# A cached-attention decode kernel: some rows of the second attention's key products go from VectorE to GpSimd and ScalarE

## The chip, the cores and the metric

One core of one Trainium2 chip. The metric is device microseconds of one execution, as the median of several runs. VectorE is DVE in the profile, ScalarE is ACT, GpSimd is POOL, TensorE is PE, and SP (SyncE) issues nearly all transfers.

## The reference, cut to what matters

Two tokens (one for each of two batch entries) go through attention, a gated MLP, the same attention and the same MLP, with the same caches and weights both times, in fp32:

```
q = (layernorm(x) @ wq).reshape(B, Sq, H, Dh).transpose(0, 2, 1, 3)     # B 2, Sq 1, H 32, Dh 128
p = softmax(einsum("bhqd,bhkd->bhqk", q, k_cache) * Dh ** -0.5)         # Sk 8192
x = x + einsum("bhqk,bhkd->bhqd", p, v_cache).reshape(B, Sq, H * Dh) @ wo
x = x + (gelu(layernorm(x) @ w_gate) * (layernorm(x) @ w_up)) @ w_down
```

Keys and values are 268 MB each, so two attentions load about 1.07 GB of the 1.15 GB that the page counts.

## The kernel before, in words

**Items and parts.** The 64 (batch, head) pairs are cut into 34 items: items 0 to 29 hold two neighbouring heads of one batch entry, items 30 to 33 one head (`ITEMS`, L60). A part is `JC` = 16 cache rows of 128 elements on each of 128 partitions: 2048 elements a partition, 1 MiB. A two-head item has 8 parts of keys and 8 of values, a one-head item 4 and 4. The first attention takes the items from 0 to 33, the second from 33 to 0 (`seq`, L498), so that keys of 32 and 33 and values of 31 to 33, still in memory from the first, aren't loaded again.

**Memory.** One buffer, `space`, is cut into 6 slots of 4 parts; the last one is shared with a ring of four weight places. `Arena` hands out ranges while the program is built. `queue` holds the loads in the order in which `plan_first`, `plan_mlp` and `plan_second` put them there; a load goes out when its range is free, and none passes another, since all are issued by SP in order (`load`, L163). So one load whose range is still in use holds up all that stand behind it.

At the start of the second attention (`plan_second`, L343) come `wq` in nine pieces, item 31's keys into the ring, item 30's keys part by part into the places of item 33's, then item 30's values, item 29's keys and item 28's keys, each into places that items 33, 32 and 31 give up, then item 29's values into the pair of slots 0 and 1 (8 MiB in one load, L362). Slot 0 holds item 30's keys and slot 1 its values until then. After that keys and values of the next items alternate, 8 MiB each, into pairs of slots.

**One part of keys** (`multiply`, L520, and `add_up`, L541). VectorE multiplies all 16 rows with the query, which stands in PSUM (`qp`) on all partitions, in place (L527). GpSimd adds the second half of each row's 128 products to the first (L539), and VectorE sums the 64 that are left into the score `S` (L542). In the first six items of the second attention ScalarE sums rows 12 to 15 itself, by an activation with an accumulator (L532), and GpSimd and VectorE do the other twelve (`own_rows`, L512). For the first and last part of the very first item (`at_once`, L516) GpSimd is left out, and VectorE sums the 12 rows over all 128 elements. `add_up` then frees the part, once ScalarE has read it too.

**Behind the keys.** `peak` (L554) takes the maximum on VectorE and transposes it on TensorE, `highest` reduces it and spreads it again over the partitions, `softmax` (L574) takes the exponents on ScalarE, `total` (L595) sums them on TensorE and inverts on VectorE (L606 for one head, L601 for two), `values` (L617) multiplies weights and value rows on TensorE into `acc` (L628) and frees the value parts, `gather` (L638) and `context` (L648) collect the result, and `divide` (L655) scales it into `oT` on VectorE (L660 or L669).

**The order.** The loop from L699 writes it out: while item n's parts are multiplied, the sums, maximum, softmax and values of the item before it, and gather, context and divide of the one before that, are put between them at fixed parts. Every engine works its instructions off in this order, so an instruction that waits holds up all behind it on its engine. The sums of part k-1 come behind the multiply of part k. `divide` comes at k = 3 (L741).

Of the kernel before, what the change touches and what calls it, by code (L numbers as in the profile page):

```python
# [9 lines left out]
F32 = mybir.dt.float32  # L10
# [5 lines left out]
P = 128  # L16
# [8 lines left out]
JC = 16  # L25
# [97 lines left out]
def decode_layers(ctx, tc, x_in, kc, vc, wq, wo, wg, wu, wd, out):  # L123
# [44 lines left out]
    def cache(key, src, n, slots=None, pieces=None):  # L168

        parts = ITEMS[n].parts  # L170

        def make():
            at = arena.pair(key) if slots is None else arena.slots(key, slots, parts)
            if at is None:
                return False
            lo = 0
            for m in pieces or (parts,):
                load(at[lo], n, src, lo, lo + m)
                lo += m
            ready[key] = dict(enumerate(map(part, at)))  # L180
            places[key] = at
            return True

        queue.append(make)

    def half(key, src, n, k, slot):

        def make():
            at = arena.slots(key, (slot,), 4, k)
            if at is None:  # L190
                return False
            load(at[0], n, src, k, k + 4)
            ready.setdefault(key, {}).update((k + i, part(a)) for i, a in enumerate(at))
            return True

        queue.append(make)
# [146 lines left out]
    def plan_second():  # L343
        for us in WQ[1]:
            half_rows(("wq", 1, us[0]), wq, us, None)
        last = PAIRS - 1
        k63, v63, k62, v62 = ("k", 1, SINGLE[3]), ("v", 1, SINGLE[3]), ("k", 1, SINGLE[2]), ("v", 1, SINGLE[2])
        for k in range(4):
            one(("k", 1, SINGLE[1]), kc, SINGLE[1], k, None)
        for k in range(4):  # L350
            one(("k", 1, SINGLE[0]), kc, SINGLE[0], k, (k63, k))

        for kind, k in (("v", 0), ("v", 1), ("k", 0), ("v", 2), ("v", 3), ("k", 1), ("k", 2), ("k", 3)):
            if kind == "k":
                one(("k", 1, last), kc, last, k, (k62, k))
            else:
                one(("v", 1, SINGLE[0]), vc, SINGLE[0], k, (v63, k))
        for k in range(4):
            one(("k", 1, last), kc, last, 4 + k, (v62, k))
        half(("k", 1, last - 1), kc, last - 1, 0, 5)  # L360
        half(("k", 1, last - 1), kc, last - 1, 4, 4)
        cache(("v", 1, last), vc, last)  # L362
        for n in range(last - 2, -1, -1):
            cache(("k", 1, n), kc, n)
            cache(("v", 1, n + 1), vc, n + 1)
        cache(("v", 1, 0), vc, 0, None, (4, 2, 1, 1))
        for g in groups(1):
            out_rows(1, g)
# [111 lines left out]
    def attention(layer):  # L480
# [19 lines left out]
        def query(n):  # L500

            it = ITEMS[n]
            qb[n] = psum2.tile([P, DH], F32, name="qp")
            for i in range(it.heads):
                h, to = it.h + i, slice(i * HALF, i * HALF + P // it.heads)
                c, r = (h // 4) % 4, h // 16 * B + it.b
                nc.tensor.matmul(  # L507
                    qb[n][to, :], pick[32 * c:32 * c + 4, r:r + 1].to_broadcast([4, P // it.heads]),
                    qsb[32 * c:32 * c + 4, (h % 4) * DH:(h % 4 + 1) * DH], start=True, stop=True,
                )  # L510

        def own_rows(n):  # L512

            return 12 if layer == 1 and n in seq[:6] else JC

        def at_once(n, k):  # L516

            return layer == 1 and n == seq[0] and k in (0, ITEMS[n].parts - 1)

        def multiply(n, k):  # L520

            if k == 0:
                S[n] = work.tile([P, SK * 2 // P], F32, name="S")
            u = t = ready[name("k", layer, n)][k]
            if layer == 0 and n in KEYS_HELD:
                u = ready["products"][k % 2]
            nc.vector.tensor_tensor(  # L527
                out=u, in0=t, in1=qb[n].unsqueeze(1).to_broadcast([P, JC, DH]), op=ALU.mult
            )
            r = own_rows(n)  # L530
            for j in range(r, JC):
                nc.scalar.activation(  # L532
                    u[:, j, :], u[:, j, :], AF.Copy, accum_out=S[n][:, k * JC + j:k * JC + j + 1]
                )
            if at_once(n, k):
                prod[n, k] = u[:, :r, :]
                return
            half = prod[n, k] = u[:, :r, :DH // 2]
            nc.gpsimd.tensor_tensor(out=half, in0=half, in1=u[:, :r, DH // 2:], op=ALU.add)  # L539

        def add_up(n, k):  # L541
            nc.vector.tensor_reduce(  # L542
                out=S[n][:, k * JC:k * JC + own_rows(n)], in_=prod.pop((n, k)), axis=AX.X, op=ALU.add
            )
            if layer == 0 and n in KEYS_HELD:
                if n == N - 1 and k >= 2:
                    done(("products", k - 2))
                return
            key = name("k", layer, n)
            done((key, k))  # L550
            if k == ITEMS[n].parts - 1:
                ready.pop(key)
# [102 lines left out]
        def divide(n):  # L655
            it = ITEMS[n]
            lo = 32 * (it.h % GH)
            r = rinv[n]
            if it.heads == 1:
                nc.vector.tensor_tensor(  # L660
                    out=oT[lo:lo + 32, it.h // GH, :, :, :],
                    in0=po[lo:lo + 32, :, :].unsqueeze(2).to_broadcast([32, GH, 2, B]),
                    in1=r[lo:lo + 32, :].unsqueeze(1).unsqueeze(1).to_broadcast([32, GH, 2, B]),
                    op=ALU.mult,
                )
                return
            for i in range(2):
                to = lo + 32 * i
                nc.vector.tensor_tensor(  # L669
                    out=oT[to:to + 32, it.h // GH, :, :, it.b],  # L670
                    in0=po[lo:lo + 32, :, i:i + 1].to_broadcast([32, GH, 2]),
                    in1=r[lo:lo + 32, i:i + 1].unsqueeze(1).to_broadcast([32, GH, 2]),
                    op=ALU.mult,
                )
# [20 lines left out]
        for lo, hi in ((lead, lead + 2), (2 - lead, 4 - lead)):  # L695
            nc.scalar.activation(qsb[:, lo * DH:hi * DH], acc[:, 0, lo * DH:hi * DH], AF.Copy, scale=rstd)
            if lo == lead:
                query(seq[0])
        for i, n in enumerate(seq):  # L699
            last = i == N - 1  # L700
            if not last:
                query(seq[i + 1])
            p = seq[i - 1] if i else None

            v = {N - 2: None, N - 1: N - 3}.get(i, i - 1) if layer == 0 else i - 1
            a = seq[i - 2] if i > 1 and completes(i - 2) and not (layer == 0 and last) else None

            soon = layer == 1 and i in (1, 4)
            first = layer == 1 and i == 1
            if first:  # L710
                add_up(p, ITEMS[p].parts - 1)
                peak(p)
                highest(p)
                softmax(p)
            for k in range(ITEMS[n].parts):
                multiply(n, k)
                if at_once(n, k) and k == 0:
                    add_up(n, k)
                if k == 1 and first:
                    values(v)  # L720
                    total(p)
                if k == 0 and p is not None and not first:
                    add_up(p, ITEMS[p].parts - 1)
                    peak(p)
                if k == (0 if soon else 1) and p is not None and not first:
                    highest(p)
                    softmax(p)
                if k == 2 and not first:
                    if p is not None:
                        total(p)  # L730
                    if a is not None:
                        gather(a)
                        if p < PAIRS:
                            context(a)
                    if v is not None and v >= 0:
                        values(v)
                    if a is not None and p >= PAIRS:
                        context(a)
                if k > 0 and (n, k - 1) in prod:
                    add_up(n, k - 1)  # L740
                if k == 3 and a is not None:  # L741
                    divide(a)
        n, p = seq[-1], seq[-2]
        add_up(n, ITEMS[n].parts - 1)
        first, second = groups(layer)[:2]
# [128 lines left out]
```

## Time and profile before

| | us |
|---|---|
| median of 3 runs | 2698.55 (2697.79 to 2700.42) |
| the profiled execution | 2699.86 |
| its span, first to last instruction | 2698.0 |
| DVE busy | 1865.5 (69%) |
| POOL busy | 1189.3 (44%) |
| PE busy | 897.0 (33%) |
| ACT busy | 130.9 (5%) |

Transfers: 1155.41 MB, 428 GB/s over the span. In the views, a line is named by its number (L527) and a buffer by the program's name; every part of keys or values is `space`. In a view of instructions the first number is the start and the second the length, in us from the start of the span; in the chain a piece is what the end waited for at that moment. The second attention's first multiply starts at 1394.57 us.

### The profile page before, as it was taken

Reading aid. Unit: us, or ns where it says so; the run is one execution under the profiler, and the core shown is the slowest. Engines: PE = TensorE matmul, PEld = TensorE weight load, DVE = VectorE, ACT = ScalarE, POOL = GpSimd, SP = SyncE. Lnnn points to the kernel's source line nnn. Section 1 sums busy time; section 2 is a strip of 40 time slices with the busy share of each in tenths; the row PEclk is TensorE's granted clock in tenths of the full one; section 3 lists DMA queues with packets and bytes.
Section 4 is the critical chain, followed back from the end, with each engine's and each line's share of the span. In section 5 each row is a group of like instructions: output and inputs, shape, how many; then the busy total and the mean of one; then the engine's idle time right before and its main releaser. Section 6 shows DMA issues by size and latency. Waiting matters only on the chain.

```text
span 2698.0 us, 18267 instructions
## 1 busy us (share of the span) xinstructions
PE 897.0 (33%) x7020; PEld 293.9 (11%) x7020; DVE 1865.5 (69%) x1688; ACT 130.9 (5%) x657; POOL 1189.3 (44%) x526
## 2 busy tenths in 40 slices
PE   1323332333233223334653332333233323322355
PEld 0100010001000000111211110001000100000022
DVE  4877787678777776876039887778767867787740
ACT  0000000000000000000013100000000000000000
POOL 2644454445445444544015454445444544544420
PEclk7656665665666566666666665666566666656667
DMA  9999999999999999999999999999999999999998
GB/s 420 436 433 433 434 435 433 432 433 435 434 433 433 432 432 432 433 429 422 407 388 409 434 428 433 433 435 431 432 435 434 431 435 432 434 434 434 435 420 379
DMA packets 33687, 1155.41 MB, mean 428 GB/s; under 512 B 4008, under 2 KB 4032, under 8 KB 5824
## 3 DMA queue, kind: packets, MB, share of 16 engines
q1 hardware_dynamic: 33560, 1154.24, 99.5%
q8 instruction: 55, 0.90, 0.1%
q14 instruction: 32, 0.26, 0.0%
q10 hardware_dynamic: 40, 0.01, 0.0%
HBM read 1154.23 MB, written 0.00 MB: 428 GB/s over the span
## 4 chain that ended last, share of the span: by engine, by line
DMA 84%; DVE 13%; PE 2%; issue 1%; POOL 0%; SPq 0%; ACT 0%; ACTq 0%; DVEq 0%; POOLq 0%
DMA space<-in_A_k_cache_dram 75%; DVE space L527 8%; DVE S L542 4%; DMA space<-in_B_w_up_dram 3%; DMA space<-in_A_wo_dram 2%; DMA space<-in_A_v_cache_dram 2%; DMA space<-in_B_w_down_dram 2%; DMA space<-in_A_wq_dram 1%; PE acc L628 0%; POOL space L539 0%; DMA space<-in_B_w_gate_dram 0%; PE acc L782 0%; DMA x<-in_A_x_dram 0%; PE acc L487 0%; PE xps L831 0%
## 5 line engine op out<-in xcount | busy, mean ns | idle before, releaser
L539 POOL TENSOR_TENSOR space<-space 128x1024 f32<-128x1024 f32 (+1 forms) x510 | 1185.3, 2324 | 1269.1 <-DVE space L527 1253.2
L527 DVE TENSOR_TENSOR space<-space,qp 128x2048 f32<-128x2048 f32 x512 | 1166.3, 2278 | 597.1 <-DMA space<-in_A_k_cache_dram 571.8
L628 PE MATMUL acc<-space,prz 128*8 128x512 f32 x4096 | 589.0, 738 | 455.7 <-DMA space<-in_A_v_cache_dram 450.9
L542 DVE TENSOR_REDUCE S<-space 128x16 f32<-128x1024 f32 (+1 forms) x512 | 612.4, 1196 | 3.1 <-POOL space L539 3.1
L558 PE MATMUL mT<-ident,m 128*1 128x128 f32 x68 | 25.0, 367 | 806.0 <-DVE m L556 806.0
L628 PEld LDWEIGHTS acc<-space,prz 128*8 128x8 f32 x4096 | 118.0, 103 | 869.4 <-DMA space<-in_A_v_cache_dram 451.8
L587 ACT ACTIVATE nbs<-nb 64x1 f32<-64x1 f32 (+1 forms) x128 | 21.1, 165 | 2230.7 <-PE nb L566 2230.0
L558 PEld LDWEIGHTS mT<-ident,m 128*1 128x1 f32 x68 | 5.4, 79 | 822.9 <-issue 791.7
L653 PE MATMUL po<-of,osb 128*32 128x2 f32 x512 | 41.0, 202 | 130.8 <-DVE osb L644 130.8
L566 PE MATMUL nb<-m,unit 1*128 1x2 f32 (+1 forms) x136 | 39.4, 357 | 124.9 <-DVE m L564 124.9
L473 POOL TENSOR_TENSOR rstd<-ve,mhalf 128x1 f32<-128x1 f32 x4 | 2.2, 550 | 167.0 <-DVE ve L471 167.0
L644 DVE SCALAR_TENSOR_TENSOR osb<-acc,diag,osb 128x128 f32<-128x128 f32 x192 | 67.4, 351 | 6.8
L807 DVE STREAM_TRANSPOSE o<-o 128x288 f32<-128x288 f32 x4 | 2.8, 693 | 92.4 <-ACT o L805 92.4
L598 PE MATMUL tot<-sums,unit 128*128 128x2 f32 x120 | 35.3, 363 | 91.7 <-ACT prz L589 91.7
L507 PE MATMUL qp<-qsb,pick 4*64 4x128 f32 (+1 forms) x256 | 31.3, 306 | 80.1 <-DVE space L527 76.9
L589 ACT ACTIVATE prz<-S,nbs 64x128 f32<-64x128 f32 (+1 forms) x128 | 50.7, 396 | 11.7 <-POOL prz L579 7.5
L653 PEld LDWEIGHTS po<-of,osb 128*32 128x32 f32 x512 | 35.7, 154 | 139.1 <-DVE osb L644 137.8
L566 PEld LDWEIGHTS nb<-m,unit 1*128 1x128 f32 x136 | 33.5, 304 | 146.3 <-DVE m L564 146.3
L477 DVE TENSOR_TENSOR x<-xps,x 128x144 f32<-128x144 f32 x4 | 1.2, 308 | 69.0 <-PE xps L831 39.1
L532 ACT ACTIVATE space<-space 128x128 f32<-128x128 f32 x128 | 38.0, 297 | 64.5 <-DVE space L527 60.8
L598 PEld LDWEIGHTS tot<-sums,unit 128*128 128x128 f32 x120 | 30.1, 312 | 96.9 <-ACT prz L589 96.9
L782 PE MATMUL acc<-space,xt 128*8 128x288 f32 x288 | 31.4, 581 | 18.4 <-DMA space<-in_B_w_up_dram 10.7
(64 smaller groups left out, 345.6 us busy)
## 6 DMA issues: line engine op xcount, KB each, us to landing
space<-in_A_k_cache_dram SPq DMA_DIRECT2D x6, 4096.0 KB
space<-in_A_v_cache_dram SPq DMA_DIRECT2D x6, 4096.0 KB
space<-in_A_wo_dram SPq DMA_DIRECT2D x15, 1152.0 KB
space<-in_A_k_cache_dram SPq DMA_DIRECT2D x16, 1024.0 KB
space<-in_B_w_gate_dram SPq DMA_DIRECT2D x3, 3456.0 KB
space<-in_A_v_cache_dram SPq DMA_DIRECT2D x10, 1024.0 KB
space<-in_A_wq_dram SPq DMA_DIRECT2D x3, 3072.0 KB
space<-in_B_w_gate_dram SPq DMA_DIRECT2D x16, 576.0 KB
```

The costliest lines, as they stand in the source:

```text
L507: nc.tensor.matmul(qb[n][to, :], pick[32 * c:32 * c + 4, r:r + 1].to_broadcast([4, P // it.heads]), qsb[32 * c:32 * c + 4, (h % 4) * DH:(h ...
L527: nc.vector.tensor_tensor(out=u, in0=t, in1=qb[n].unsqueeze(1).to_broadcast([P, JC, DH]), op=ALU.mult)
L532: nc.scalar.activation(u[:, j, :], u[:, j, :], AF.Copy, accum_out=S[n][:, k * JC + j:k * JC + j + 1])
L539: nc.gpsimd.tensor_tensor(out=half, in0=half, in1=u[:, :r, DH // 2:], op=ALU.add)
L542: nc.vector.tensor_reduce(out=S[n][:, k * JC:k * JC + own_rows(n)], in_=prod.pop((n, k)), axis=AX.X, op=ALU.add)
L566: nc.tensor.matmul(mT[n][:, :heads], ones[0:1, :], m1[:, :heads], start=True, stop=True)
L589: nc.scalar.activation(pr[at, lo:].rearrange("p (g e) -> p g e", e=4)[:, 0:it.rows // 2:2, :], s[at, :it.rows].rearrange("p (g r) -> p g r ...
L598: nc.tensor.matmul(tot[:, :it.heads], ones, rs.pop(n), start=True, stop=True)
L628: nc.tensor.matmul(accumulator(n)[32 * c:32 * c + 8, :], pr[:, at:at + 8], t[g // 4][:, g % 4 * 4:g % 4 * 4 + 4, :].rearrange("p j d -> p ...
L644: nc.vector.scalar_tensor_tensor(t, q[:, r, :], diag[:, r:r + 1], t, op0=ALU.mult, op1=ALU.add,)
L653: nc.tensor.matmul(po[lo:lo + 32, i, :], t[:, i::GH], of, start=True, stop=True)
L782: nc.tensor.matmul(acc[32 * c:32 * c + 4 * B, h, :HG], window(u, 4 * g + 2 * e), w[:, k, c, :], start=(key == steps[0][0] and k == 0), sto ...
```

## The change

In the first five items of the second attention (33 to 29) VectorE multiplies rows 0 to 11 of each part, and GpSimd rows 12 to 15. GpSimd doesn't read PSUM, so ScalarE first copies the item's query to `qs` in SBUF, once an item. ScalarE sums rows 9 to 15, GpSimd and VectorE rows 0 to 8; in the two `at_once` parts ScalarE sums rows 11 to 15 and VectorE the other 11. Item 28, which had ScalarE's help before, has none now. Item 29's values come as two loads, parts 0 to 3 into slot 0 and parts 4 to 7 into slot 1, and each waits for its own slot only. Where the item before the one at hand has one head, `divide` moves from k = 3 to k = 1 of the next item (`late`); in the first attention this concerns item 29, in the second item 32.

```diff
-        cache(("v", 1, last), vc, last)
+        half(("v", 1, last), vc, last, 0, 0)
+        half(("v", 1, last), vc, last, 4, 1)
...
-        def own_rows(n):
-
-            return 12 if layer == 1 and n in seq[:6] else JC
+        def waited(n):
+
+            return layer == 1 and n in seq[:5]
...
+        def own_rows(n, k):
+
+            return 11 if at_once(n, k) else 9 if waited(n) else JC
+
+        qs = once.tile([P, 2, DH], F32, name="qs", tag="xc")
...
+            rows = 12 if waited(n) else JC
             nc.vector.tensor_tensor(
-                out=u, in0=t, in1=qb[n].unsqueeze(1).to_broadcast([P, JC, DH]), op=ALU.mult
+                out=u[:, :rows, :], in0=t[:, :rows, :], in1=qb[n].unsqueeze(1).to_broadcast([P, rows, DH]), op=ALU.mult
             )
-            r = own_rows(n)
+            if rows < JC:
+                q = qs[:, n % 2, :]
+                if k == 0:
+                    nc.scalar.copy(q, qb[n])
+                nc.gpsimd.tensor_tensor(
+                    out=u[:, rows:, :], in0=t[:, rows:, :], in1=q.unsqueeze(1).to_broadcast([P, JC - rows, DH]),
+                    op=ALU.mult,
+                )
+            r = own_rows(n, k)
...
+        late = None
         for i, n in enumerate(seq):
...
-                if k == 3 and a is not None:
+                if k == 3 and a is not None and p < PAIRS:
                     divide(a)
+                if k == 1 and late is not None:
+                    divide(late)
+            late = a if a is not None and p >= PAIRS else None
```

`half` (L186), used before for item 28's keys, loads four parts of an item into one slot.

More of the change, by code (lines that the diff above doesn't have):

```diff
@@ L542, in add_up @@
             nc.vector.tensor_reduce(
-                out=S[n][:, k * JC:k * JC + own_rows(n)], in_=prod.pop((n, k)), axis=AX.X, op=ALU.add
+                out=S[n][:, k * JC:k * JC + own_rows(n, k)], in_=prod.pop((n, k)), axis=AX.X, op=ALU.add
             )
```

## The prediction

> **What bounds the kernel now.** I read the page's chain and slices first, then windows over the start of the second attention, then the chain and SP's issues there.
>
> ```profile
> GB/s 420 436 433 433 434 435 433 432 433 435 434 433 433 432 432 432 433 429 422 407 388 409 434 428 433 433 435 431 432 435 434 431 435 432 434 434 434 435 420 379
> ...
> DMA 84%; DVE 13%; PE 2%; issue 1%; POOL 0%; SPq 0%; ACT 0%; ACTq 0%; DVEq 0%; POOLq 0%
> ```
>
> Most of the chain is loading, near one rate. The slices dip in the middle (429 to 388, between 1147 and 1484 us) and at the end. The edit concerns the stretch from 1390 on. The windows view gives its rate in the last column; the first two rows are the steady stretches on either side:
>
> ```profile
> 100.00:1200.00 1100.00, 335.55 (x2309) 103.87 (x2309) 824.55 (x717) 38.03 (x174) 537.23 (x228) 0.61 1.00 433
> 1560.00:2500.00 940.00, 279.59 (x1948) 86.26 (x1952) 701.26 (x607) 31.48 (x144) 456.48 (x194) 0.62 1.00 433
> ...
> 1390.00:1400.00 10.00, 3.11 (x12) 1.03 (x12) 5.39 (x3) 2.12 (x10) 0.00 (x0) 0.56 0.98 405
> 1400.00:1410.00 10.00, 1.40 (x5) 0.84 (x5) 9.43 (x9) 3.83 (x24) 3.63 (x2) 0.50 0.74 270
> 1410.00:1420.00 10.00, 6.20 (x36) 1.48 (x36) 7.11 (x5) 3.18 (x19) 3.65 (x2) 0.75 0.96 354
> 1420.00:1430.00 10.00, 1.24 (x4) 0.66 (x4) 9.90 (x10) 4.12 (x26) 5.62 (x4) 0.59 1.01 419
> 1430.00:1440.00 10.00, 6.67 (x40) 2.03 (x40) 9.96 (x8) 4.85 (x33) 6.09 (x4) 0.72 0.99 376
> 1440.00:1450.00 10.00, 4.17 (x21) 1.67 (x25) 9.83 (x12) 3.52 (x23) 4.61 (x3) 0.62 1.06 444
> 1450.00:1460.00 10.00, 5.48 (x39) 2.12 (x29) 6.57 (x8) 3.17 (x19) 3.62 (x2) 0.67 0.99 429
> 1460.00:1470.00 10.00, 6.82 (x34) 1.29 (x34) 10.00 (x9) 3.99 (x25) 5.51 (x4) 0.67 0.83 330
> ```
>
> The eight short rows add to 3027; times 10 us that is 30.3 MB, where 433 GB/s would bring 34.6. The missing 4.37 MB are **10.1 us** of lost loading: all that this change can win here. VectorE (third column) is busy 68 of these 80 us.
>
> Who holds the loads back shows in SP's issues (start, length), taken one by one:
>
> ```profile
> 1398.72 0.33 SPq L166 DMA_DIRECT2D space<-in_A_k_cache_dram  x1
> ...
> 1403.98 0.33 SPq L166 DMA_DIRECT2D space<-in_A_k_cache_dram  x1
> ...
> 1413.01 0.33 SPq L166 DMA_DIRECT2D space<-in_A_v_cache_dram  x1
> ...
> 1418.05 0.33 SPq L166 DMA_DIRECT2D space<-in_A_k_cache_dram  x1
> ...
> 1434.06 0.33 SPq L166 DMA_DIRECT2D space<-in_A_k_cache_dram  x1
> ...
> 1440.03 0.33 SPq L166 DMA_DIRECT2D space<-in_A_k_cache_dram  x1
> ...
> 1453.59 0.33 SPq L166 DMA_DIRECT2D space<-in_A_k_cache_dram  x1
> 1466.94 0.33 SPq L166 DMA_DIRECT2D space<-in_A_v_cache_dram  x1
> 1482.96 0.33 SPq L166 DMA_DIRECT2D space<-in_A_k_cache_dram  x1
> ```
>
> By the order of `plan_second` these are: key parts 0 and 1 of item 30 (each waits for the sums of a part of item 33), value part 0 of item 30 (for item 33's values), key parts 0 and 4 of item 29, the two halves of item 28's keys (for item 31's last sums, and for its values), the values of item 29, 8 MiB in one load (for item 30's keys and values), the keys of item 27. The chain (start, length) gives a part's two VectorE steps, and what follows:
>
> ```profile
> 1447.26 6.23 PE acc L628 x32
> ...
> 1467.62 2.20 DVE space L527
> 1469.81 0.86 DVE S L542
> ...
> 1482.96 25.67 DMA space<-in_A_k_cache_dram
> 1508.66 2.29 DVE space L527
> ...
> 1511.88 36.01 DMA space<-in_A_k_cache_dram
> ```
>
> A MiB takes 2.42 us at 433 GB/s, 8 MiB take 19.4. Item 27's keys take 25.7 us from issue, since item 29's values are still loading; the next take 36. So the queue never runs dry after 1466.94, and whatever item 27's keys land earlier than 1508.63, the end comes earlier too.
>
> **The change, part by part.** The durations, mean ns of one, from the groups by form over 1384 to 1550 us:
>
> ```profile
> L527 DVE TENSOR_TENSOR space<-space,qp 128x2048 f32<-128x2048 f32 x41 | 93.1, 2275 | 32.4 <-PE qp L507 22.1 <-DMA space<-in_A_k_cache_dram 10.2
> L539 POOL TENSOR_TENSOR space<-space 128x768 f32<-128x768 f32 x30 | 54.5, 1816 | 80.9 <-DVE space L527 72.4 <-DMA space<-in_A_k_cache_dram 3.2 <-issue 2.8
> ...
> L532 ACT ACTIVATE space<-space 128x128 f32<-128x128 f32 x128 | 38.0, 297 | 64.5 <-DVE space L527 60.8 <-issue 3.7
> L542 DVE TENSOR_REDUCE S<-space 128x12 f32<-128x768 f32 x30 | 28.2, 938 | 0.0
> ...
> L539 POOL TENSOR_TENSOR space<-space 128x1024 f32<-128x1024 f32 x8 | 18.9, 2358 | 12.2 <-DVE space L527 12.2
> L542 DVE TENSOR_REDUCE S<-space 128x16 f32<-128x1024 f32 x7 | 8.5, 1211 | 0.0
> ```
>
> VectorE, per part: the two sums differ by 273 ns over 256 elements, 1.07 ns an element. Twelve rows of a multiply save 512 elements, 0.55 us; nine rows of a sum instead of twelve save 192, 0.20. In the chain a part takes 2.20+0.86 = 3.06, so 1.65+0.66 = **2.31** after.
>
> GpSimd, per part: 542 ns over 256 elements is 2.12 ns an element, with 0.19 fixed. The half-addition of 576 elements is 1.41. No row shows GpSimd multiplying a row block. Bounds: 0.55, VectorE's own time for these rows, and 2.5, twice the addition's. I take the addition's 0.19+512x2.12 = 1.27, the nearest row. With two gaps, **2.74** a part: less than VectorE's 3.06 now, more than its 2.31 after. GpSimd becomes the bound wherever VectorE has no other work.
>
> The Trainium skill, GPSIMD Engine Reference, section 4.1 (Engine selection), speaks against this move: ordinary elementwise work belongs on VectorE, since two-input operations on GpSimd are about twice as slow. The rows here agree (1.27 against 0.55); by the rule alone the gain would be the second case below, by the rows it depends on 2.74 being under 3.06.
>
> ScalarE sums seven rows, 7x0.297 and the last read, 2.3 us, under GpSimd's 2.74. The new copy of `qp` to `qs`, 128x128 elements as in a row's sum (0.30), I put at 0.35 us (0.30 to twice that, as it reads PSUM); it comes once an item, ahead of GpSimd's first multiply, and costs nothing where that item's part isn't the next due. Behind it on ScalarE stand that part's sums, for which the freeing of the part waits.
>
> Now the stretch, laid out in order, engine by engine, with these durations. Item 33: multiply 1.65, sum of 11 rows 0.86+640x1.07 ns = 1.54 (from 1394.57 to 1397.8), two multiplies and a sum to 1401.9, where key part 1 of item 30 goes out, **2.1** earlier. Its last sums end at 1405.9, ScalarE's at 1406.4 behind GpSimd's multiply, so peak and weights follow 2.3 earlier, and with them item 30's value part 0 at 1410.2 (**2.8** earlier). Item 32 then waits for TensorE's total:
>
> ```profile
> DVE rinv L606 <- PE tot L598: 2.9, 1, 2.9
> DVE oT L660 <- PE po L653: 2.8, 1, 2.8
> ```
>
> Two shorter multiplies reach that wait sooner, so it grows to 4.2, and key part 0 of item 29 gains **2.3** only. Item 32 then runs at GpSimd's 2.7 a part; its weights wait on ScalarE behind item 31's part 1, and key part 4 of item 29 comes at 1430.6 (**3.5**). Item 31: item 28's first half at 1434.9 (**5.1**), the second at 1449.1 (**4.5**; the same gather, then TensorE's 6.2 us of values). The second row is the wait for item 32's context; `late` moves this divide to the next item, past it. But then VectorE comes earlier to item 30's maximum, whose transpose stands behind item 31's values on TensorE: a new wait of 2.1, so of 2.8 little is left. Item 30's keys end at 1448.2, the first half of item 29's values goes straight behind item 28's second half (1449.5), the other at 1459.3 (before: both at 1466.94). Item 29's eight parts at 2.74: item 27's keys at 1471.2 (**11.8**), now 9.6 ahead of a dry queue.
>
> What is left of the idle time: I charge 1.9 us from an issue into an empty queue until its transfer counts, an estimate; laid out so, the kernel before lands item 27's keys at 1508.0 (1508.63 measured), with its issues within 0.8 of the rows. Afterwards the queue is dry 1.5 us before item 30's key part 1, 0.9 before its value part 0, 0.7 and 0.3 before item 29's key parts 0 and 4, 0.2 elsewhere: **3.6**, none later. Against the measured 10.1 that is 6.5 won; the two layouts against each other give 7.8 (1508.0 to 1500.2). I take 7.2.
>
> The separate loads alone, without the rows, would win 3.0 (only the last gap closes); with the rows they add nearly nothing, since item 30's values then end in time for one load too. Item 28 loses ScalarE's help: eight parts at 3.3 instead of 3.06, 2 us, inside a slack of 19 before its buffers are due. In the first attention `late` moves one divide out of a wait:
>
> ```profile
> 1228.84 0.32 DVE L669 TENSOR_TENSOR oT<-po,rinv 32x8 f32<-32x8 f32 x2 [2.16 <-PE po L653]
> 1231.42 2.29 DVE L527 TENSOR_TENSOR space<-space,qp 128x2048 f32<-128x2048 f32 x1 [2.26 <-issue]
> ```
>
> It now falls into the busy stretch after 1231: between nothing and its own 0.32 lost, or more only if a load waits for it. I take nothing, since most of the chain is loading.
>
> **How the numbers follow.** The profiled execution took 2699.86 us, its span 2698.0; the median of the three runs is 2698.55, and I subtract from that. 0.2% (5.4 us) is about what a measurement of this kernel tells from no change.
>
> - **Forecast**, 0.64: 2698.55-7.2 = **2691.4**, own range 2688.4 (all 10.1 won) to 2693.
> - **GpSimd binds harder**, 0.24: its pair of instructions takes 3.5 us (1.3 times). Item 29's eight parts and the weights waiting on ScalarE then eat the gain; the layout leaves 2.7: 2695.8. For it: no row of such a multiply, and GpSimd nearly without pause. Against: the row below.
> - **GpSimd slower than VectorE was**, 0.09: a pair over 3.65 us, past VectorE's old 3.06 with the old waits, makes the chain from item 33 to item 29 longer than before. At 4.0 us the layout loses 7.5: 2706. The mechanism would be its multiply costing over 1.75 times the addition, or both engines slowing each other at the memory. Against it, GpSimd's times (min, median, max) are nearly alike whatever VectorE did beside it:
>
> ```profile
> L539 POOL TENSOR_TENSOR space<-space x510: 1804/2351/2393, 46.9 to 2585.8; 128x1024 f32<-128x1024 f32 x160, 128x768 f32<-128x768 f32 x10
> ```
>
> The Trainium skill, GPSIMD Engine Reference, section 1 (Specifications), has GpSimd share its SBUF interfaces with VectorE when that reads two SBUF inputs; the multiply's second input is `qp` in PSUM, so by it the case would be rarer still; no run here tests it yet.
> - **The split isn't one**, 0.03: VectorE's multiply is made to wait for GpSimd's of the same part, as both write one buffer. Each part then takes the sum of both, and the layout loses 23: 2721. Against it, ScalarE and GpSimd already work on rows of one part side by side:
>
> ```profile
> 1400.88 0.31 ACT L532 ACTIVATE space<-space 128x128 f32<-128x128 f32 x1 [2.70 <-DVE space L527]
> 1400.92 1.82 POOL L539 TENSOR_TENSOR space<-space 128x768 f32<-128x768 f32 x1 [27.82 <-DVE space L527]
> ```
>
> Up to 2698.0 the range holds the first two cases, 0.88, less their tails: about 0.83. Faster by over 0.2% is nearly all of the forecast, 0.62; the second case and the forecast's poor end make 0.26 within; the last two 0.12.
>
> **What would show it.** Right: GpSimd's two groups at 1.27 and 1.41; the 1400 to 1470 windows near 400 and more; item 27's keys landing at 1500 to 1502; VectorE waiting for GpSimd by 0.3 to 0.5 a part in item 29. Wrong: a GpSimd multiply over 1.7, a copy to `qs` that holds GpSimd up, item 27's keys issued after 1480, or a dry queue past 1470.

## The result, and the profile after

| | before | after |
|---|---|---|
| median, 22 runs each | 2698.68 us | 2694.40 us |
| ratio, 95% interval | | 0.9984 (0.9978 to 0.9990) |
| span of the profiled execution | 2698.0 us | 2693.0 us |

The change wins **4.3 us**, 0.16%; 7.2 was forecast. The lines of the changed kernel are up to 20 further down: L535 is VectorE's multiply, L542 GpSimd's, L555 GpSimd's half-addition, L558 VectorE's sum, L548 ScalarE's sum, L622 the inverse of a total.

The slices and the chain on the page after:

```profile
GB/s 421 436 435 433 435 430 434 434 430 435 433 431 434 435 435 432 431 428 425 403 405 422 438 432 434 434 433 433 433 431 437 430 434 431 435 435 436 428 423 373
...
DMA 79%; PE 12%; DVE 7%; POOL 1%; issue 1%; ACT 0%; SPq 0%; ACTq 0%; POOLq 0%; DVEq 0%
```

The two slices from 1349 to 1484 us, 388 and 409 GB/s before, are now 405 and 422 (a slice is 67 us long). The start of the second attention in windows of 10 us, with the rate in the last column and GpSimd's and ScalarE's busy times ahead of the clock:

```profile
1390.00:1400.00 10.00, 2.20 (x20) 0.62 (x12) 5.82 (x4) 3.43 (x18) 3.19 (x3) 0.73 1.01 424
1400.00:1410.00 10.00, 3.53 (x17) 1.49 (x21) 8.83 (x9) 6.78 (x44) 5.66 (x5) 0.50 0.99 364
1410.00:1420.00 10.00, 4.60 (x32) 1.32 (x23) 6.69 (x8) 6.88 (x45) 8.89 (x8) 0.84 0.99 365
1420.00:1430.00 10.00, 3.83 (x17) 1.50 (x21) 8.41 (x10) 8.11 (x52) 9.06 (x8) 0.50 1.01 423
1430.00:1440.00 10.00, 4.81 (x33) 1.42 (x25) 8.48 (x13) 8.56 (x56) 8.83 (x8) 0.84 1.02 424
1440.00:1450.00 10.00, 8.12 (x53) 2.83 (x57) 8.31 (x11) 6.05 (x39) 7.31 (x7) 0.67 1.04 443
1450.00:1460.00 10.00, 4.85 (x32) 0.77 (x24) 9.89 (x11) 9.06 (x59) 9.71 (x8) 0.84 1.03 438
1460.00:1470.00 10.00, 1.06 (x5) 0.37 (x5) 9.54 (x9) 6.24 (x40) 9.48 (x7) 0.50 0.99 427
```

From 1420 on loading runs at its steady rate; 270 became 364 at 1400, and 354 only 365 at 1410. GpSimd, busy for 3.6 to 6.1 of each 10 us from 1400 on before, is at nine tenths in most of these windows. SP's issues of the loads that the prediction followed:

```profile
1401.62 0.33 SPq L166 DMA_DIRECT2D space<-in_A_k_cache_dram  x1
...
1410.14 0.33 SPq L166 DMA_DIRECT2D space<-in_A_v_cache_dram  x1
...
1414.76 0.33 SPq L166 DMA_DIRECT2D space<-in_A_k_cache_dram  x1
...
1429.59 0.33 SPq L166 DMA_DIRECT2D space<-in_A_k_cache_dram  x1
...
1433.99 0.37 SPq L166 DMA_DIRECT2D space<-in_A_k_cache_dram  x1
1446.96 0.33 SPq L166 DMA_DIRECT2D space<-in_A_k_cache_dram  x1
1447.39 0.37 SPq L166 DMA_DIRECT2D space<-in_A_v_cache_dram  x1
1454.92 0.33 SPq L166 DMA_DIRECT2D space<-in_A_v_cache_dram  x1
1468.45 0.33 SPq L166 DMA_DIRECT2D space<-in_A_k_cache_dram  x1
```

Against the forecast (1401.9, 1410.2, 1415.8, 1430.6, 1434.9, 1449.1, 1449.5, 1459.3, 1471.2) each is on time or up to 4.4 us early. Item 27's keys were issued 14.5 us sooner than before, and yet landed only 4.7 sooner, as VectorE's first multiply of them shows (1508.66 before; 1500 to 1502 was named as a sign of being right):

```profile
1503.92 2.29 DVE L535 TENSOR_TENSOR space<-space,qp 128x2048 f32<-128x2048 f32 x1 [8.65 <-DMA space<-in_A_k_cache_dram]
```

So the issues came as laid out or earlier; how much idle loading that closes, and how much of it comes out at the end, was mis-sized. For that I use one figure from here on: the rate over 1390 to 1510 us. Loading lost is 120 us times its shortfall from 433, over 433 (between 1100 and 1390 us it is summed over windows of 10 us). The kernel before, in its first trace:

```profile
1390.00:1510.00 120.00, 48.12 (x265) 17.18 (x265) 106.03 (x89) 45.20 (x276) 54.74 (x31) 0.62 0.97 399
...
1500.00:1510.00 10.00, 2.03 (x17) 0.49 (x8) 9.00 (x7) 3.83 (x24) 5.45 (x3) 0.69 1.12 486
```

and the changed one:

```profile
1390.00:1510.00 120.00, 45.73 (x274) 15.27 (x266) 95.96 (x94) 56.43 (x353) 81.42 (x56) 0.66 1.01 421
```

That is 9.4 lost before and 3.3 after: 6.1 closed. (The prediction's 10.1 stopped at 1470; the 486 GB/s from 1500 on in this trace make up for part of it.)

### The profile page after: what moved, and what is told of

Its sections match the earlier page's. It is cut to its first block, busy times and chain, and to the rows that moved or that the text cites. A ratio compares the mean times of both kernels' runs of the same rounds, so it can differ in the third digit from the quotient of the medians.

```text
span 2693.0 us, 18383 instructions
## 1 busy us (share of the span) xinstructions
PE 899.8 (33%) x7020; PEld 292.9 (11%) x7020; DVE 1850.8 (69%) x1688; ACT 142.2 (5%) x734; POOL 1213.6 (45%) x550
## 4 chain that ended last, share of the span: by engine, by line
DMA 79%; PE 12%; DVE 7%; POOL 1%; issue 1%; ACT 0%; SPq 0%; ACTq 0%; POOLq 0%; DVEq 0%
DMA space<-in_A_k_cache_dram 39%; DMA space<-in_A_v_cache_dram 32%; PE acc L644 10%; DVE space L535 4%; DVE S L558 2%; DMA space<-in_B_w_down_dram 2%; DMA space<-in_A_wo_dram 2%; DMA space<-in_B_w_gate_dram 2%; DMA space<-in_B_w_up_dram 1%; POOL space L555 1%; DMA space<-in_A_wq_dram 1%; PE xps L851 0%; PE acc L802 0%; DMA x<-in_A_x_dram 0%; POOL space L542 0%
## 5 line engine op out<-in xcount | busy, mean ns | idle before, releaser
L555 POOL TENSOR_TENSOR space<-space 128x1024 f32<-128x1024 f32 (+1 forms) x510 | 1180.7, 2315 | 1208.1 <-DVE space L535 1197.2
L535 DVE TENSOR_TENSOR space<-space,qp 128x2048 f32<-128x2048 f32 (+1 forms) x512 | 1153.5, 2253 | 604.2 <-DMA space<-in_A_k_cache_dram 579.1
L644 PE MATMUL acc<-space,prz 128*8 128x512 f32 x4096 | 595.3, 745 | 456.3 <-DMA space<-in_A_v_cache_dram 451.3
L558 DVE TENSOR_REDUCE S<-space 128x16 f32<-128x1024 f32 (+1 forms) x512 | 609.8, 1191 | 4.1 <-POOL space L555 3.9
L548 ACT ACTIVATE space<-space 128x128 f32<-128x128 f32 x164 | 48.5, 297 | 14.1 <-DVE space L535 7.8
L542 POOL TENSOR_TENSOR space<-space,qs 128x512 f32<-128x512 f32 x24 | 30.5, 1271 | 29.2 <-ACT qs L541 26.8
```

What stands on the lines that cost most here:

```text
L535: nc.vector.tensor_tensor(out=u[:, :rows, :], in0=t[:, :rows, :], in1=qb[n].unsqueeze(1).to_broadcast([P, rows, DH]), op=ALU.mult)
L542: nc.gpsimd.tensor_tensor(out=u[:, rows:, :], in0=t[:, rows:, :], in1=q.unsqueeze(1).to_broadcast([P, JC - rows, DH]), op=ALU.mult,)
L548: nc.scalar.activation(u[:, j, :], u[:, j, :], AF.Copy, accum_out=S[n][:, k * JC + j:k * JC + j + 1])
L558: nc.vector.tensor_reduce(out=S[n][:, k * JC:k * JC + own_rows(n, k)], in_=prod.pop((n, k)), axis=AX.X, op=ALU.add)
L644: nc.tensor.matmul(accumulator(n)[32 * c:32 * c + 8, :], pr[:, at:at + 8], t[g // 4][:, g % 4 * 4:g % 4 * 4 + 4, :].rearrange("p j d -> p ...
```

## The experiments

Theory A: the gain is the idle loading closed, and what is left after 1400 us is the wait for the parts of items 33 and 32. The rivals: the two loads bring it (B), the moved divide costs something in the first attention (C), ScalarE's share brings it and not GpSimd's multiply (D), loads of one MiB are slow by themselves (E), GpSimd's pace is what is missing (F).

**The two loads alone.**

```diff
-        cache(("v", 1, last), vc, last)
+        half(("v", 1, last), vc, last, 0, 0)
+        half(("v", 1, last), vc, last, 4, 1)
```

> The kernel before with item 29's values as two loads, nothing else. Theory A (the gain is the idle time closed between 1400 and 1470 us, and the loads and the rows close the same last gap): the laid-out sum gives 3.0, scaled by what the whole change brought against its sum (4.3 of 7.8) 1.7: 1.5 to 3.0 us faster. Rival B (the two loads bring most of the gain): 3.5 to 4.5 faster.

2698.44 us against 2699.84: ratio 0.9994 (0.9985 to 1.0003).

```profile
1390.00:1510.00 120.00, 47.58 (x265) 17.11 (x265) 107.06 (x90) 45.20 (x276) 54.71 (x31) 0.62 0.99 409
```

6.7 lost, so 2.7 closed, near the 3.0 laid out; 1.4 of time, just under what A said. The interval, from 0.8 slower to 4.0 faster, holds no change as well as B's 3.5, so this run alone settles neither.

**The moved divide alone.**

```diff
-                if k == 3 and a is not None:
+                if k == 3 and a is not None and p < PAIRS:
                     divide(a)
+                if k == 1 and late is not None:
+                    divide(late)
+            late = a if a is not None and p >= PAIRS else None
```

> The kernel before with the moved divide, nothing else. Theory A: VectorE's wait of 2.8 us for item 32's context goes, item 30's values end some 3 us earlier: 1.5 to 3.0 us faster. Rival C (the divide moved in the first attention delays the loads there and costs 0.7 to 1.5 us, which is why the whole change brought less than forecast): 0 to 1.5 faster, and the first multiply of the second attention starts later than 1394.6 by that much.

2698.34 us: 0.9995 (0.9987 to 1.0004), 1.5 less, on the border between A and C, and not told from no change by time. Its first multiply came at 1393.4, not later than 1394.6, which speaks against C.

```profile
1390.00:1510.00 120.00, 46.91 (x270) 16.53 (x266) 108.70 (x92) 45.20 (x276) 56.31 (x32) 0.63 0.99 409
```

6.7 lost here too, 2.7 closed.

**The rows alone** (the changed kernel with the first diff undone, and the second).

> The changed kernel with one load for item 29's values and the divide at its old place. Theory A: 5.7 by the laid-out sum, 3.1 scaled: 3 to 5 us faster. Rival B: under 1 faster. Rival C: as fast as the whole change or faster, 4.3 to 5.5.

2694.21 us against 2699.84: 0.9980 (0.9971 to 0.9989), 5.6 less.

```profile
1390.00:1510.00 120.00, 47.21 (x270) 14.88 (x266) 96.13 (x94) 56.25 (x353) 81.32 (x56) 0.64 1.00 418
```

The rows by themselves are as fast as the whole change, within what the intervals tell, and by 0.6 us faster than A had said at most; C had allowed for that. Item 32's divide still waits there for its context, 3.5 us where it was 2.8:

```profile
DVE rinv L621 <- PE tot L613: 5.7, 3, 3.2
DVE oT L675 <- PE po L668: 3.5, 1, 3.5
```

**The rows and the moved divide, one load** (the first diff undone).

> The changed kernel with one load for item 29's values. Theory A: item 30's values end in time for one load, so it is as fast as the whole change, 3.8 to 4.8 us faster than before. Rival B: 0 to 1 faster.

2694.70 us: 0.9982 (0.9974 to 0.9991), 5.1 less, a little above A's 4.8.

```profile
1390.00:1510.00 120.00, 46.55 (x268) 15.04 (x268) 97.54 (x95) 56.46 (x354) 82.73 (x57) 0.61 1.01 422
```

3.0 lost, as with two loads (3.3 and 3.9). B is out: beside the rows, the two loads add nothing that the runs tell.

**The changed kernel again.**

> The changed kernel once more, unaltered. The first comparison gave 4.3 us, its traces 5.0. Theory A (6.2 us of idle loading closed in the stretch, and what is missing to that is drift elsewhere that differs from execution to execution): 4.3 to 5.5 us faster, with the loading lost between 1100 and 1390 us anywhere from 7.5 to 9 us. Rival C (the edit itself costs loading before 1390): that loss is again at 8.8, over 1 us above the kernel before.

2694.16 us against 2699.62: 0.9981 (0.9972 to 0.9990), 5.5 less, 3.9 lost in the stretch. From 1100 to 1390 it lost 8.2, where the first traces had 7.7 (before) and 8.8 (after).

```profile
1390.00:1510.00 120.00, 47.49 (x274) 15.69 (x266) 95.74 (x92) 56.42 (x353) 81.49 (x56) 0.63 1.00 419
```

**All rows multiplied by VectorE.**

```diff
-            rows = 12 if waited(n) else JC
+            rows = JC
```

> The changed kernel, but VectorE multiplies all 16 rows itself and GpSimd none; ScalarE still sums seven. Theory A (a part takes 2.85 us on VectorE then, 2.74 on GpSimd with its multiply): the idle time left is 6.4 instead of 3.6, so 2 to 3 us slower than the changed kernel, 1.5 to 3 faster than before. Rival D (ScalarE's larger share brings the gain, GpSimd's multiply nothing): within 0.7 of the changed kernel.

2697.77 us against 2699.62: 0.9995 (0.9986 to 1.0003). Of 5.5 us, 1.9 are left, so D is out: GpSimd's multiply carries most of the gain (3.6 us slower without it, where A had said 2 to 3).

```profile
1390.00:1510.00 120.00, 44.64 (x273) 15.82 (x273) 105.36 (x90) 54.83 (x348) 50.84 (x32) 0.67 1.00 413
```

**Three rows for GpSimd** (`rows = 13`).

> The changed kernel, with three rows multiplied by GpSimd instead of four: a part takes 2.41 us on VectorE and 2.47 on GpSimd. Theory A: 0.4 us less idle time, too little to tell from the changed kernel; item 27's keys are issued 0.5 to 1 us earlier. Rival F (GpSimd's pace per part is what is missing to the forecast): over 1 us faster than the changed kernel.

2694.51 us: 0.9981 (0.9972 to 0.9990), the same as the changed kernel. F is out. Item 27's keys went out at 1469.4, not earlier as expected, and the stretch lost more in this trace, 5.0:

```profile
1390.00:1510.00 120.00, 45.49 (x266) 15.47 (x266) 97.48 (x92) 55.91 (x353) 75.09 (x56) 0.63 1.00 415
```

**The total of item 33 later.**

```diff
                 if k == 1 and first:
                     values(v)
-                    total(p)
...
                     add_up(n, k - 1)
+                if k == 2 and first:
+                    total(p)
```

> The changed kernel, with item 33's total put behind the sums of item 32's part 1 instead of ahead of those of part 0, so that VectorE frees part 0 of item 32 before it waits for TensorE. Theory A: key part 0 of item 29 goes out at about 1412.5 instead of 1414.8, the queue's gaps before it and before key part 4 close, 1.0 by the laid-out sum: 0.5 to 1.3 us faster than the changed kernel. Rival E (loads of one MiB issued one by one are slow whatever VectorE does, so the loss between 1400 and 1420 stays): no different from the changed kernel, the loss there at 3.1.

2694.51 us: 0.9980 (0.9971 to 0.9989), nothing to tell from the changed kernel, though item 29's key part 0 went out at 1411.32 instead of 1414.76. (All of this trace lies 1.0 earlier from its first multiply on, so 2.4 of that are the edit's.) The two windows are hardly better:

```profile
1400.00:1410.00 10.00, 4.56 (x21) 1.66 (x25) 8.36 (x8) 6.61 (x43) 5.66 (x5) 0.50 1.00 372
1410.00:1420.00 10.00, 3.46 (x25) 0.97 (x17) 8.91 (x10) 8.43 (x54) 9.77 (x9) 0.84 0.98 370
```

This is a miss of A as I had laid it out, and a point for E.

**Items 33 and 32 cut short**, to part A from E.

```diff
-            rows = 12 if waited(n) else JC
+            rows = 4 if light(n) else 12 if waited(n) else JC
...
-            if rows < JC:
+            if rows == 12:
...
-            for j in range(r, JC):
+            for j in range(r, r if light(n) else JC):
```

(`light` holds for the first two items of the second attention; `S` is set to zero first, and `own_rows` is 4 there.)

> The changed kernel, with the scores of items 33 and 32 cut short: four rows of each part are multiplied and summed, on VectorE and GpSimd, ScalarE sums none, and the other scores are set to zero, so that the first parts come free up to 8 us earlier. Its values are loaded and used as before. Theory A (what is still lost after 1400 is the wait for those parts): the queue never runs dry, the loss between 1390 and 1510 falls from 3 or 4 us to under 1, and it is 2 to 3.6 us faster than the changed kernel, 7 to 9 faster than before. Rival E (loads of one MiB lose this time themselves): the loss stays at 2.5 to 3.5, and it is less than 1 us faster than the changed kernel.

2691.34 us against 2699.77: 0.9970 (0.9959 to 0.9982), **8.4** less. The two windows:

```profile
1400.00:1410.00 10.00, 6.73 (x37) 1.83 (x37) 3.50 (x10) 0.61 (x3) 2.13 (x3) 0.70 1.01 419
1410.00:1420.00 10.00, 3.22 (x15) 1.64 (x19) 8.06 (x11) 7.08 (x46) 8.32 (x7) 0.64 1.01 421
...
1390.00:1510.00 120.00, 47.73 (x276) 14.80 (x268) 86.81 (x95) 40.76 (x252) 70.23 (x51) 0.66 1.02 432
```

The same loads of one MiB, issued 2.5 to 6 us earlier (item 30's key part 0 at 1396.41 instead of 1398.91, item 29's at 1408.49 instead of 1414.76), run at 420 GB/s, and 0.3 us is lost in place of 3 or 4. Nor do busy engines slow the loads: from 1410 on they work here about as much as in the changed kernel, at 421 GB/s instead of 365. E is out: what the changed kernel still loses after 1400 is the wait for the parts of items 33 and 32.

**The kernel before, twice more, and the first attention's divide put back.** Two more traces of the kernel before:

> The kernel before, unaltered, for a second trace. Theory A: the loading lost between 1390 and 1510 us is again 9 to 10.5 us, that between 1100 and 1390 anywhere from 7.5 to 9. Rival C: the latter again at 7.7.

> The kernel before, unaltered, for a third trace. Theory A: loading lost between 1100 and 1390 us anywhere from 7.2 to 9.2. Rival C: under 7.8 again. Both: 9 to 10.5 lost between 1390 and 1510.

They lost 10.0 and 8.9 us in the stretch (rates of 397 and 401), so 9.4 on average with the first, and 7.2 and 8.0 between 1100 and 1390. The changed kernel with `late` for the second attention only:

```diff
-                if k == 3 and a is not None and p < PAIRS:
+                if k == 3 and a is not None and (p < PAIRS or layer == 0):
...
-            late = a if a is not None and p >= PAIRS else None
+            late = a if a is not None and p >= PAIRS and layer == 1 else None
```

> The changed kernel with the first attention's divide at its old place, so that nothing differs from the kernel before until the second attention's first multiply. Loading lost between 1100 and 1390 us so far: 7.7 and 7.2 in two traces of the kernel before, 7.7 to 9.2 in those of the others. Theory A (that loss drifts from execution to execution): anywhere from 7.2 to 9.2, and as fast as the changed kernel. Rival C (the moved divide costs it): 7.2 to 7.7, and 0.7 to 1.2 us faster than the changed kernel.

2694.39 us against 2699.04: 0.9983 (0.9974 to 0.9992), 4.7 less, so no faster than the changed kernel, though this trace lost only 6.9 between 1100 and 1390, less than either theory had said. The rows of the stretch before 1390, of this kernel first:

```profile
1100.00:1390.00 290.00, 137.40 (x1359) 46.34 (x1347) 134.99 (x155) 8.33 (x36) 81.73 (x40) 0.69 1.00 423
```

and of the third trace of the kernel before:

```profile
1100.00:1390.00 290.00, 136.68 (x1351) 47.70 (x1343) 135.35 (x156) 8.32 (x36) 81.76 (x40) 0.68 1.00 421
```

That loss drifts between executions, from 7.2 to 8.0 with the kernel before alone. Over all kernels kept, those whose program up to the second attention's first multiply is that of before (the three traces, the two loads alone, the rows alone, this one) lost 6.9 to 8.4, and those with the moved divide 7.6 to 9.3, half a microsecond more on average. But the first multiply starts no later in the latter (1393.1 to 1395.1, against 1394.0 to 1395.1). C's 0.7 to 1.5 us is not borne out; a cost of half a microsecond isn't excluded.

## Why the prediction was right, and where its size was off

**What bounds the stretch: right, and shown.** Freeing the parts of items 33 and 32 sooner closes the lost loading and takes the time with it (8.4 us when nearly all of it goes). Of the parts of the change taken singly, the rows bring far more (5.6 us) than the two loads (1.4) or the divide (1.5), in the order laid out.

**The durations: right.** The groups by form in the changed kernel (mean ns of one):

```profile
L535 DVE TENSOR_TENSOR space<-space,qp 128x1536 f32<-128x1536 f32 x24 | 41.8, 1744 | 20.4 <-PE qp L508 20.0 <-ACT qs L541 0.3
...
L555 POOL TENSOR_TENSOR space<-space 128x576 f32<-128x576 f32 x22 | 31.0, 1411 | 3.4 <-DVE space L535 3.1 <-POOL space L542 0.3
...
L542 POOL TENSOR_TENSOR space<-space,qs 128x512 f32<-128x512 f32 x24 | 30.5, 1271 | 29.2 <-ACT qs L541 26.8 <-DVE space L535 1.3 <-issue 1.2
...
L558 DVE TENSOR_REDUCE S<-space 128x9 f32<-128x576 f32 x22 | 16.4, 746 | 1.0 <-POOL space L555 0.8
```

GpSimd's multiply, which no row had shown, takes 1.27 us, its addition 1.41, as estimated from the addition's slope. The second, third and fourth case (GpSimd's pair at 3.5 us or more, or the two multiplies in turn in every part) didn't come; the fourth row's wait shows what GpSimd as the bound costs VectorE, 0.8 us in all, less than the 0.3 to 0.5 a part that I expected. In item 29 two multiplies of GpSimd start 2.59 apart (not 2.74, as its instructions overlap a little: 1.27 and 1.41 make 2.68):

```profile
1459.51 1.27 POOL L542 TENSOR_TENSOR space<-space,qs 128x512 f32<-128x512 f32 x1
...
1462.10 1.27 POOL L542 TENSOR_TENSOR space<-space,qs 128x512 f32<-128x512 f32 x1
```

**The new waits: in part.** VectorE's waits over 1394 to 1484 (total, number, longest):

```profile
DVE rinv L622 <- PE tot L614: 5.7, 3, 3.3
DVE m L580 <- PE mT L574: 2.0, 2, 1.6
```

The wait behind item 31's values is there (1.6, 2.1 forecast). The wait for item 33's total, 2.9 in the trace that the prediction read and 3.1 and 3.5 in the other two before, is 3.3 and not 4.2. The first row holds two more waits, 1.3 and 1.1, for the totals of items 32 and 31, that neither the prediction nor the kernel before had.

**The copy to `qs`: wrong.** It was put at 0.35 us and at no cost. It takes 0.27, but in each of the five items it starts within 0.04 us of the end of VectorE's multiply of the first part, and GpSimd's multiply of that part starts behind it. Item 32's:

```profile
1406.75 1.73 DVE L535 TENSOR_TENSOR space<-space,qp 128x1536 f32<-128x1536 f32 x1
...
1408.52 0.27 ACT L541 COPY qs<-qp 128x128 f32<-128x128 f32 x1 [0.38 <-DVE space L535]
...
1408.86 1.28 POOL L542 TENSOR_TENSOR space<-space,qs 128x512 f32<-128x512 f32 x1 [4.34 <-ACT qs L541]
```

So an item's first part does take both multiplies in turn. In item 33 ScalarE's sums of the first part stand behind GpSimd's multiply, and item 30's key part 0 goes out no sooner than before (1398.91, 1398.72 before). The prediction had named a copy that holds GpSimd up as a sign of being wrong; what the order costs in all, no run shows.

**The two loads, item 28, the first attention's divide: right.** The loads add nothing beside the rows, as priced; item 28 without ScalarE's help still leaves VectorE 8.65 us of waiting for item 27's keys; `late` adds nothing that the runs tell either, though I had let it pass as worth little, not nothing.

**The step that failed: "what is left of the idle time", and with it the 7.2.** I weighed 10.1 (windows to 1470) against the 11.4 that lie behind the layout's 7.8, and took 7.2 closed. By the rates over 1390 to 1510, three traces of the kernel before lost 9.4 on average, and two of the changed one 3.3 and 3.9 (3.6 forecast), so 6.1 and 5.5 were closed. By that count what was left was right, and what was there before was put too high. How the two share the error hangs on the count, though. A window counts a packet's bytes where the packet starts; spread over the packets' recorded times, the stretch lost 11.1, 11.1 and 10.3 before and 4.1 and 4.7 after, 6.4 closed on average. By either count the closed time is smaller than 7.2.

And I counted each microsecond closed as one won, with nothing for what the rest of the execution loses. Over the eleven comparisons above the time won adds to 48.6 us and the loading closed, from 9.4, to 57.9. That would be 0.84 for one, but such a factor is not shown: a straight line through the eleven has a slope of 1.03 and lies 1.0 us lower. The traces show where most of the difference lies. The eleven spans are 51.6 us shorter in sum than the mean of the three before, and between 1100 and 1390 us these traces lost about 5 more in sum. For the changed kernel, 6.1 and 5.5 were closed, 1.2 and 0.6 more lost before 1390 (8.8 and 8.2, against 7.6 on average before), so 4.9 is left in both; its spans are 4.9 and 5.3 shorter, and the comparisons gave 4.3 and 5.5.

Right by its sign and its mechanism, the forecast lay beyond the interval (2.7 to 5.9 us), and most of its chance was put on more than 0.2%, where the first comparison gave 0.16%. Its own range ended at 2693; 2694.40 lies in the wider one, up to 2698.0, mainly by the room that was given to a slower GpSimd, which didn't come. That much is luck. Of the signs that it named, the two groups of GpSimd came; the windows at 1400 and 1410 (364 and 365), item 27's landing and VectorE's waits for GpSimd did not.

**Open.** Whether the greater loss before 1390 in the changed kernels' traces is drift or in part a cost of the moved divide. Why the copy to `qs` waits for VectorE's multiply, as both only read `qp`. And why the earlier issue in the kernel with the later total closed no more than it did (2.8 lost in its trace, against 3.3 and 3.9).

## What to carry to other kernels

In a kernel bound by loading, take the lost loading from several traces over a stretch that ends in steady loading, and expect losses elsewhere to shift the time by a microsecond or so. The parts that free the first buffers set what is lost; edits further along that chain (the two loads, the moved divide here) close the same gap, and their gains didn't add up here. Rows given to an engine that was half idle paid here, even at more than twice the cost per row (1.27 us for four rows, against 0.53 on VectorE), as its 2.59 us per part stayed under VectorE's old 3.06.

## What the hardware showed that I had not expected

GpSimd's multiply of 512 elements with a broadcast second operand took 1.271 us beside VectorE's, with no sign of one slowing the other: VectorE's twelve rows took 1744 ns, where 2275 for sixteen less 512x1.07 gives 1727, and the half-addition 1411 with GpSimd busy nine tenths of the time and 1409 in the kernel where it multiplied nothing:

```profile
L555 POOL TENSOR_TENSOR space<-space 128x576 f32<-128x576 f32 x22 | 31.0, 1409 | 69.0 <-DVE space L535 65.5 <-DVE rinv L622 1.8 <-DMA space<-in_A_k_cache_dram 1.7
```

The Trainium skill, GPSIMD Engine Reference, section 1 (Specifications), names contention with VectorE's instructions that run in a 2-port mode or read two SBUF inputs. VectorE's multiply here reads one, the other stands in PSUM, and the trace agrees with 1271 and 1411 ns beside it; no run here was made with two.
